# Four groups of layer-two weights kept in DRAM as float32, low parts reordered, and one head's load moved ahead

## The chip, the cores and the metric

The kernel runs on one core of a Trainium2 chip. Its engines have queues of their own, and each works its queue in order: PE (TensorE, matmuls; PEld is its weight loading), DVE (VectorE), ACT (ScalarE), POOL (GpSimd), and SP (SyncE), which issues nearly all DMAs here. The metric is the time of one execution on the device in microseconds (us), the median of several runs.

## The reference

Attention with a decay over 4 batches of 8 heads, 576 positions and 64 values a head, then two feed-forward layers over the 2304 tokens:

```python
scores = scale * q @ k.T + (cum[:, None] - cum[None, :])     # cum: cumulative sum of log(f), causal
x = softmax(scores) @ v                                       # (2304, 512)
h = x @ w_in;   x = (h * clip(h + 3, 0, 6) / 6) @ w_out       # layer one, w_in 512 x 2048
h = x @ w_in2;  y = (max(h, 0) + alpha * min(h, 0)) @ w_out2  # layer two
```

The weights of both layers arrive as float64 bit patterns (two 32-bit words for each number), everything else as float32; the output is float32.

## The kernel before

**Layout.** The hidden width of 2048 is cut into 8 groups of 256; the tokens into three parts of 768 (`p` = 0, 1, 2). A *set* is one layer, one group and one part (`sets`, lines 619 to 625). In each layer the sets with p = 0 and 1 come first, group by group, and then the eight sets with p = 2 in the order 6, 7, 0 to 5. These last eight are the "last third" of a layer.

**A set in steps.** The order inside a set is written out by hand. `SEQ` (line 597) is a string: a digit is one of seven products of a Strassen scheme (`product`, six matmuls each) of this set's tokens with the input weights, a `q` is one `piece` (six matmuls) of the set before with the output weights. A layer-one set has 15 steps, a layer-two set 13. The sums of products and the activation (`activate`: ACT, DVE, ACT and POOL in turn) follow one or two steps later. PSUM holds two tiles for the products of bank A and one each for B and C, so a product waits until ACT (line 687) or DVE (line 690) has read the one before.

**High and low parts.** Matmuls work on a rounded float32 form. Each operand is a pair: the high part is a rounding copy on ACT, the low part is what the copy lost, a subtraction on POOL or DVE. For input weights that is line 176 (`high`) and line 180 (`low`), in four blocks named a, b, c, d (a: columns 0 and 1, used by the products 1 and 7; c: 4 and 5; d: 6; b: 2 and 3), for output weights o0 and o1. For the activations it is line 226 and line 231 (`build_parts`): seven blocks 0 to 6, some of which are sums made on line 223. The products use the blocks in the order 0, 3, 6, 2, 4, 1, 5.

**Conversion of the weights.** A group has four slices (two of input, two of output weights) of 128 x 512 numbers. `fetch` (line 114) brings the raw 512 KB. Then come `m` (magnitude, ACT, line 132), `f`, `s`, `j`, `g` (floor, shift, join, sign; DVE, lines 135 to 148) which make a float32 slice in one of three buffers (`wa`, `wb`, `wc`); `S1` to `S4` (POOL, line 162) make the Strassen sums, and `h..` and `l..` the high and low parts; `wi0` to `wo1` store both to DRAM (line 185), from where the last third loads them (`load_w`, lines 208 and 210). `sign` issues the fetch two slices on.

**Side work by tables.** The strings `CONV_...` and `BUILD` give each of these a step. `side_work` (line 739) is called at the start of a set and queues them with `aside`; in each step the products' own work comes first, then the side work due. The weights of a layer-two group are converted during the two sets of the group before it by `CONV_EVEN`, shifted by 3 steps: 26 steps in all. Those of its first group are converted by `CONV_A` and `CONV_TURN` in the last sets of layer one and the first of layer two.

**The start.** `load_head` brings q and k of one head (608 KB, three buffers) and, for even heads, v. `ak_d` and `aq_d` are copies in DRAM of the rows that carry the decay; from head 2 on `prep_head` reads them back (lines 295 and 296).

Of the kernel before, what the change touches and what calls it, by code (L numbers as in the profile page):

```python
# [21 lines left out]
def decay_attention_ffn2_kernel(ctx, tc, qk, v, f, wi1, wo1, wi2, wo2, alpha, out):  # L22
    nc = tc.nc
# [15 lines left out]
    KT = 5  # L39
    TAIL = S - 512  # L40
# [9 lines left out]
    CONV_EVEN = "m0 0 f0 1 s0 2.5 j0 4 g0 5.5 m1 5 f1 7 s1 8.5 j1 10 g1 11.5 S1 12 S2 13 hc 14 S3 14 hb 15 lc 15 lb 16 ha 16 S4 17 m2 18 hd 18 f2 19 ld 19 s2 20 la 20 j2 21 m3 21 g2 22.5 f3 23 ho0 23 lo0 24 s3 24.5 j3 26 g3 27 ho1 28 lo1 29 wi0 40 wi1 43 wo0 46 wo1 48"  # L50
    CONV_TURN = "S1 11 S3 12 S2 13 hb 30 ha 30 hc 31 lb 32 la 33 S4 34 lc 35 m2 38 hd 37 ld 38 f2 41 s2 42 j2 43 g2 44 m3 42 f3 46 s3 47 j3 48 g3 49 ho0 47 lo0 49 ho1 51 lo1 52 wi0 58 wi1 61 wo0 64 wo1 66"
# [27 lines left out]

    aq_d = dram.tile([2, 32, 4, QW], F32, name="aq_d")  # L80
# [35 lines left out]
    def conv_ops(ff, g):  # L116
# [3 lines left out]
        def f32(s):  # L120

            if s not in stage:
                tag = {0: "wa", 1: "wb", 2: "wc", 3: "wb", "S": "wc"}[s]
                stage[s] = wtmp.tile([128, KH, 256], F32, tag=tag, name=tag)
            return stage[s]
# [60 lines left out]

        for s in range(4):
            for name, fn in (("m", magnitude), ("f", floor), ("s", shift), ("j", join), ("g", sign)):
                ops[f"{name}{s}"] = lambda fn=fn, s=s: fn(s)
# [53 lines left out]
    def build_ops(k, p, add, subs):  # L243
        adds, highs, lows = build_parts(k, p, add, subs)
        return [(t, {"h": highs, "l": lows, "a": adds}[name[0]][int(name[1]), c])
# [14 lines left out]
    def attention():  # L260
        with ExitStack() as ax:
# [239 lines left out]
            for a in range(2):  # L501
                nc.sync.dma_start(out=ak_d[a, 0:NP], in_=ak[32 * a:32 * a + NP].bitcast(F32))
            prep_head(1)
# [14 lines left out]
            load_head(3)  # L518
# [220 lines left out]
    def side_work(s):  # L739
# [8 lines left out]
        def build(k, pair, subs, add=nc.vector, even=None):  # L748
            for i, (t, fn) in enumerate(build_ops(k, pair, add, subs)):
                aside(t if even is None else even[0] + i / even[1], fn)  # L750
# [10 lines left out]
        if p == 0 and (1 if ff else 2) <= g + 1 < NG and not (ff == 0 and g < 2):  # L761
            ops, keep = conv_ops(ff, g + 1), g + 1 < NG - 2
            for text in ((CONV_EVEN,) if ff else (CONV_A, CONV_B)):
                conversion(ops, text, keep, 1, 3 if ff else 5)
        if p == NPR - 1:
# [8 lines left out]
            if ff == 0 and j == NG - 3:  # L774
                early["second"] = conv_ops(1, 0)
                conversion(early["second"], CONV_A, True)
# [104 lines left out]
```

## Time and profile before

| | |
|---|---|
| median of 3 runs | 1024.52 us (1023.65 to 1025.59) |
| the profiled execution | 1023.57 us, of which its span is 1021.8 us |
| PE busy | 966.4 us (95%) |
| DVE, ACT, POOL busy | 739.2 (72%), 588.5 (58%), 589.0 (58%) us |
| mean granted clock of PE | 0.992 of full |
| DMA | 139.18 MB, mean 136 GB/s |

Attention takes about the first 240 us, layer one lasts until about 604 us, layer two until the end. Busy time counts an engine's own work only; a wait shows as idle time, put down to the engine that ended it. PEclk is the granted clock: 1.00 is the higher of its two levels (2.4 GHz), 0.50 the lower (1.2 GHz).

### The profile page before, as it was taken

To read this page: it belongs to the slowest core of one execution; us is meant where nothing else is said; L and a number is where in the kernel's file an instruction comes from. 1 tells how busy PE (TensorE), PEld (TensorE's weight loads), DVE (VectorE), ACT (ScalarE), POOL (GpSimd) and SP (SyncE) were. 2 spreads that over 40 slices of the span, in tenths; PEclk is the share of its full clock that TensorE was granted. 3 is DMA by queue.
4 is the path that set the end of the run, shared out by engine and by line. 5 is a ranking of instruction groups with operands and counts; after the bars stand their busy time and mean duration, and the time that the engine had idled before them with its cause. 6 is when DMAs were issued, how large, how long until landed. Compare 5 with 4: busy or idle time off the path is not lost.

```text
span 1021.8 us, 15850 instructions
## 1 busy us (share of the span) xinstructions
PE 966.4 (95%) x5488; PEld 862.7 (84%) x5488; DVE 739.2 (72%) x1284; ACT 588.5 (58%) x1444; POOL 589.0 (58%) x577
## 2 busy tenths in 40 slices
PE   4999999998999999999999997999999999999998
PEld 3666666678899999998999996888888888888987
DVE  6787987857688788878345668677887778735454
ACT  4677787776555555554544354766555556564452
POOL 7467578856655656566555377565556556532221
PEclk9899999999999999999999998999999999999999
DMA  7555576501424444210254513344244420244531
GB/s 206 178 173 153 173 241 212 149 6 42 155 71 169 181 171 181 94 43 1 76 223 179 203 53 104 131 166 175 85 174 163 167 83 0 94 170 160 226 144 73
DMA packets 32260, 139.18 MB, mean 136 GB/s; under 512 B 4156, under 2 KB 4156, under 8 KB 29044
## 3 DMA queue, kind: packets, MB, share of 16 engines
q1 hardware_dynamic: 32176, 138.17, 39.0%
q8 instruction: 43, 0.70, 0.3%
q14 instruction: 37, 0.30, 0.1%
q10 hardware_dynamic: 4, 0.00, 0.0%
HBM read 94.06 MB, written 39.94 MB: 131 GB/s over the span
## 4 chain that ended last, share of the span: by engine, by line
PE 71%; DVE 15%; POOL 5%; ACT 4%; issue 3%; DMA 1%; SPq 1%; ACTq 0%; DVEq 0%; POOLq 0%
PE o L715 17%; PE o L713 16%; PE hA L682 16%; PE hC L682 9%; PE pv L436 4%; PE hB L682 4%; DVE nm L323 3%; PE tp L379 2%; PE sc L346 2%; POOL wi L180 2%; POOL g L665 1%; DVE nm L325 1%; DVE r L223 1%; ACT g L664 1%; PE sc L347 1%
## 5 line engine op out<-in xcount | busy, mean ns | idle before, releaser
L682 PE MATMUL hA<-xh,wi 128*128 128x384 f32 x768 | 227.1, 341 | 22.2 <-POOL wi L180 11.2
L713 PE MATMUL o<-g,wo 128*128 128x384 f32 x1152 | 232.3, 340 | 1.2 <-POOL g L665 1.2
L715 PE MATMUL o<-wo,g 128*128 128x512 f32 x864 | 224.1, 395 | 1.8 <-POOL g L665 1.4
L665 POOL TENSOR_TENSOR g<-t,g 128x384 fp32r<-128x384 f32 x120 | 127.7, 1065 | 162.2 <-ACT g L664 142.5
L713 PEld LDWEIGHTS o<-g,wo 128*128 128x128 f32 x1152 | 205.8, 189 | 2.1 <-POOL g L665 1.8
L715 PEld LDWEIGHTS o<-wo,g 128*128 128x128 f32 x864 | 160.5, 188 | 29.0 <-POOL g L665 2.7
L682 PEld LDWEIGHTS hA<-xh,wi 128*128 128x128 f32 x768 | 142.1, 189 | 29.8 <-POOL wi L180 13.5
L665 POOL TENSOR_TENSOR g<-s,g 128x384 fp32r<-128x384 f32 x72 | 75.8, 1053 | 155.3 <-ACT g L664 144.9
L733 DVE TENSOR_TENSOR r<-o,r 128x512 f32<-128x512 f32 x126 | 86.5, 687 | 64.0 <-PE o L715 62.9
L682 PE MATMUL hA<-xl,wi 128*128 128x384 f32 x384 | 130.4, 340 | 2.1 <-POOL xl L231 2.1
L722 DVE SCALAR_TENSOR_TENSOR r<-o,r 128x384 f32<-128x384 f32 x168 | 91.4, 551 | 50.5 <-PE o L713 50.1
L664 ACT CAST g<-t 128x384 fp32r<-128x384 f32 x120 | 61.7, 514 | 107.4 <-DVE t L656 89.2
L682 PE MATMUL hC<-xh,wi 128*128 128x384 f32 x384 | 114.3, 338 | 1.3 <-ACT s L687 1.3
L331 ACT ACTIVATE p<-sc,nm 128x128 f32<-128x128 f32 (+4 forms) x160 | 84.5, 531 | 21.3 <-DVE nm L325 9.9
L323 DVE TENSOR_REDUCE nm<-sc 128x1 f32<-128x128 f32 (+4 forms) x160 | 71.5, 469 | 10.5 <-PE sc L348 7.8
L231 POOL TENSOR_TENSOR xl<-r,xh 128x384 fp32r<-128x384 f32 x65 | 74.8, 1168 | 5.1 <-ACT xh L226 4.9
L682 PEld LDWEIGHTS hA<-xl,wi 128*128 128x128 f32 x384 | 72.7, 189 | 5.4 <-POOL xl L231 2.3
L664 ACT CAST g<-s 128x384 fp32r<-128x384 f32 x72 | 37.0, 514 | 65.9 <-DVE s L659 65.1
L682 PEld LDWEIGHTS hC<-xh,wi 128*128 128x128 f32 x384 | 71.1, 188 | 3.8 <-ACT s L687 1.6
L687 ACT COPY s<-hA 128x384 f32<-128x384 f32 x96 | 45.9, 478 | 44.3 <-PE hA L682 44.2
L379 PE MATMUL tp<-ident,p 128*128 128x128 f32 x384 | 69.4, 285 | 0.6 <-ACT pt L395 0.6
L346 PE MATMUL sc<-k,q 128*128 128x256 f32 (+2 forms) x128 | 55.9, 437 | 11.6 <-DVE k L314 9.4
(128 smaller groups left out, 1927.2 us busy)
## 6 DMA issues: line engine op xcount, KB each, us to landing
wid<-wi SPq DMA_DIRECT2D x24, 896.0 KB
wi<-wid SPq DMA_DIRECT2D x12, 1792.0 KB
rqk<-in_qk SPq DMA_DIRECT2D x32, 608.0 KB
raw<-in_wi SPq DMA_DIRECT2D x32, 512.0 KB
raw<-in_wo SPq DMA_DIRECT2D x32, 512.0 KB
wod<-wo SPq DMA_DIRECT2D x24, 512.0 KB
wo<-wod SPq DMA_DIRECT2D x12, 1024.0 KB
vt<-in_v SPq DMA_DIRECT2D x16, 320.0 KB
```

Source lines behind the costliest of these rows:

```text
L231: e.tensor_sub(out=XS[k][1][:, b, c], in0=x, in1=XS[k][0][:, b, c].bitcast(F32))
L323: nc.vector.tensor_reduce(out=nm[:, i:i + 1], in_=src, axis=AX.X, op=ALU.max, negate=True)
L331: nc.scalar.activation(out=pt[:, c0:c0 + cw], in_=src, func=AF.Exp, bias=nm[:, 0:1], scale=1.0, accum_out=dsts[i])
L346: nc.tensor.matmul(out=sc[:, 0:n], lhsT=q1[:, qs], rhs=k1[:, 0:n], start=True, stop=False)
L379: nc.tensor.transpose(tp[:, j, :], pt[:, 128 * j:128 * j + 128], ident)
L664: nc.scalar.copy(out=gt[n][i][:, 0], in_=hold["g"])
L665: nc.gpsimd.tensor_sub(out=gt[n][i][:, 1], in0=hold["g"], in1=gt[n][i][:, 0].bitcast(F32))
L682: nc.tensor.matmul(out=h, lhsT=a, rhs=b[:, x, kc], start=new and kc + e == 0, stop=kc == KH - 1 and e == 2, skip_group_check=not new)
L713: nc.tensor.matmul(out=o[:, 0:NB], lhsT=a[:, cs], rhs=b, start=st, stop=sp)
L715: nc.tensor.matmul(out=o, lhsT=b[:, cs], rhs=a, start=st, stop=sp)
L722: later(0, lambda: nc.vector.scalar_tensor_tensor(out=acc, in0=o[:, 0:NB], scalar=1.0 / 6.0, in1=acc, op0=ALU.mult, op1=ALU.add))
L733: nc.vector.tensor_add(out=acc, in0=o, in1=acc)
```

## The change

1. In the last third of layer one, from its first set on, sixteen slices of layer two (groups 0 to 3, `NC` = 4) are converted, a slice in six steps, and stored as float32 in a new DRAM buffer `f_d` (`c0` to `c3`); the three buffers are taken in turn.
2. For these four groups `CONV_TURN` now begins with loads of those slices (`p0` to `p3`) on SP in place of the conversion, and goes on with sums, high and low parts as before. For group 0 it is queued in the last set but one of layer one.
3. `CONV_EVEN` (layer-two groups 4 to 7) runs its first slices up to 1.5 steps closer together, and the high and low part of block a come before b instead of last (`ha` 13 for 16, `la` 15 for 20).
4. Two of the builds of activations take a new order (`BUILD_FIRST`): block 6 directly after its sum, ahead of 4 and 1.
5. The load of head 3 is issued directly after the copies `ak_d`, ahead of the copies `aq_d` and of the preparation of head 1, and no longer after them.

```diff
@@ -37,6 +37,7 @@
     KT = 5
+    NC = 4
     TAIL = S - 512
@@ -47,8 +48,9 @@
     CONV_B = "hb 11 S1 11 S3 12 lb 13 S2 13 S4 14 ha 14 hc 16 la 16 hd 17 lc 18 ld 19 m2 19 f2 20 s2 21 j2 22 g2 23 m3 21 f3 24 s3 25 j3 26 g3 27 ho0 25 lo0 27 ho1 29 lo1 31 wi0 40 wi1 43 wo0 46 wo1 48"
-    CONV_EVEN = "m0 0 f0 1 s0 2.5 j0 4 g0 5.5 m1 5 f1 7 s1 8.5 j1 10 g1 11.5 S1 12 S2 13 hc 14 S3 14 hb 15 lc 15 lb 16 ha 16 S4 17 m2 18 hd 18 f2 19 ld 19 s2 20 la 20 j2 21 m3 21 g2 22.5 f3 23 ho0 23 lo0 24 s3 24.5 j3 26 g3 27 ho1 28 lo1 29 wi0 40 wi1 43 wo0 46 wo1 48"
-    CONV_TURN = "S1 11 S3 12 S2 13 hb 30 ha 30 hc 31 lb 32 la 33 S4 34 lc 35 m2 38 hd 37 ld 38 f2 41 s2 42 j2 43 g2 44 m3 42 f3 46 s3 47 j3 48 g3 49 ho0 47 lo0 49 ho1 51 lo1 52 wi0 58 wi1 61 wo0 64 wo1 66"
+    CONV_EVEN = "m0 0 f0 1 s0 2 j0 3.5 g0 5 m1 4 f1 6.5 s1 8 j1 9 g1 10 S1 11 S2 12 S3 12 hc 13 ha 13 lc 14 hb 14 la 15 lb 16 S4 17 m2 18 hd 18 f2 19 ld 19 s2 20 j2 21 m3 21 g2 22.5 f3 23 ho0 23 lo0 24 s3 24.5 j3 26 g3 27 ho1 28 lo1 29 wi0 40 wi1 43 wo0 46 wo1 48"
+    CONV_TURN = "p0 0 p1 0 S1 6 S2 7 S3 7 hc 8 ha 8 lc 9 hb 9 la 10 lb 11 S4 12 hd 13 ld 14 p2 14 p3 15 ho0 24 lo0 25 ho1 26 lo1 27 wi0 40 wi1 43 wo0 46 wo1 48"
+    BUILD_FIRST = "h0 l0 a3 h3 l3 h2 l2 a4 a6 h6 l6 h4 l4 h1 l1 a5 h5 l5"
     BUILD = "h0 2 l0 4 a3 6 h3 9 l3 11 h2 9 l2 11 a4 13 a6 15 h4 16 l4 18 h1 17 l1 19 h6 19 l6 21 a5 22 h5 26 l5 28"
@@ -77,6 +79,7 @@
+    f_d = [dram.tile([128, 4, KH * 256], F32, name=f"fd{g}") for g in range(NC)]
     aq_d = dram.tile([2, 32, 4, QW], F32, name="aq_d")
@@ -113,7 +116,7 @@
-    def conv_ops(ff, g):
+    def conv_ops(ff, g, cache=False):
@@ -121,6 +124,8 @@
                 tag = {0: "wa", 1: "wb", 2: "wc", 3: "wb", "S": "wc"}[s]
+                if cache:
+                    tag = ("wa", "wb", "wc")[(4 * g + s) % 3]
                 stage[s] = wtmp.tile([128, KH, 256], F32, tag=tag, name=tag)
@@ -184,7 +189,16 @@
+        def saved(s, put):
+            t = f32(s).rearrange("p k n -> p (k n)")
+            if put:
+                nc.sync.dma_start(out=f_d[g][:, s], in_=t)
+            else:
+                nc.sync.dma_start(out=t, in_=f_d[g][:, s])
+
         for s in range(4):
+            ops[f"c{s}"] = lambda s=s: saved(s, True)
+            ops[f"p{s}"] = lambda s=s: saved(s, False)
             for name, fn in (("m", magnitude), ("f", floor), ("s", shift), ("j", join), ("g", sign)):
@@ -240,8 +254,12 @@
-    def build_ops(k, p, add, subs):
+    def build_ops(k, p, add, subs, even=None):
         adds, highs, lows = build_parts(k, p, add, subs)
+        if even is not None:
+            fns = [{"h": highs, "l": lows, "a": adds}[name[0]][int(name[1]), c]
+                   for name in BUILD_FIRST.split() for c in range(KH)]
+            return [(even[0] + i / even[1], fn) for i, fn in enumerate(fns)]
         return [(t, {"h": highs, "l": lows, "a": adds}[name[0]][int(name[1]), c])
@@ -500,6 +518,7 @@
                 nc.sync.dma_start(out=ak_d[a, 0:NP], in_=ak[32 * a:32 * a + NP].bitcast(F32))
+            load_head(3)
             prep_head(1)
@@ -515,7 +534,6 @@
                 nc.sync.dma_start(out=aq_d[a, 0:NP], in_=aq[32 * a:32 * a + NP].bitcast(F32))
-            load_head(3)
             nc.gpsimd.tensor_scalar(out=alpha_sb, in0=alpha_sb, scalar1=-1.0, scalar2=None, op0=ALU.mult)
@@ -746,8 +764,8 @@
         def build(k, pair, subs, add=nc.vector, even=None):
-            for i, (t, fn) in enumerate(build_ops(k, pair, add, subs)):
-                aside(t if even is None else even[0] + i / even[1], fn)
+            for t, fn in build_ops(k, pair, add, subs, even):
+                aside(t, fn)
@@ -760,8 +778,9 @@
             ops, keep = conv_ops(ff, g + 1), g + 1 < NG - 2
-            for text in ((CONV_EVEN,) if ff else (CONV_A, CONV_B)):
-                conversion(ops, text, keep, 1, 3 if ff else 5)
+            cached = ff == 1 and g + 1 < NC
+            for text in ((CONV_TURN if cached else CONV_EVEN,) if ff else (CONV_A, CONV_B)):
+                conversion(ops, text, keep, 1, 3 if ff and not cached else 5)
         if p == NPR - 1:
@@ -771,12 +790,15 @@
                 build(1, 0, (nc.gpsimd,), nc.gpsimd, (0, 0.7))
-            if ff == 0 and j == NG - 3:
-                early["second"] = conv_ops(1, 0)
-                conversion(early["second"], CONV_A, True)
-                conversion(early["second"], CONV_TURN, True, last=15)
+            if ff == 0 and j == 0:
+                for k in range(4 * NC):
+                    if k % 4 == 0:
+                        ops = conv_ops(1, k // 4, True)
+                    for i, name in enumerate("mfsjgc"):
+                        aside(6 * k + (0, 1, 2, 3, 4, 5)[i], ops[f"{name}{k % 4}"])
+            if ff == 0 and j == NG - 2:
+                conversion(conv_ops(1, 0), CONV_TURN, True, 1, 7)
             if ff == 0 and j == NG - 1:
-                conversion(early["second"], CONV_TURN, True, 1, -30, 30)
                 build(0, 1, (nc.gpsimd, nc.vector), nc.gpsimd)
```

## Rows read from the trace of the kernel before

**Rows 1.** The page, its part 1: busy us (share) xinstructions.
```profile
PE 966.4 (95%) x5488; PEld 862.7 (84%) x5488; DVE 739.2 (72%) x1284; ACT 588.5 (58%) x1444; POOL 589.0 (58%) x577
```

**Rows 2.** Waits of PE: waiter and releaser, us in total, times, longest.
```profile
PE hA L682 <- POOL wi L180: 11.2, 7, 1.9
...
PE hA L682 <- DVE s L690: 7.7, 2, 5.7
PE sc L347 <- DMA k<-ak_d: 5.3, 1, 5.3
...
PE hA L682 <- POOL xl L231: 2.1, 1, 2.1
```

**Rows 3.** Windows, most cut at sets; busy (instructions), granted clock, DMA share, GB/s.
```profile
320.00:460.00 140.00, 140.00 (x799) 140.00 (x798) 117.29 (x203) 73.51 (x145) 83.91 (x79) 1.00 0.36 130
380.00:400.00 20.00, 20.00 (x115) 20.00 (x115) 18.84 (x34) 10.31 (x21) 9.34 (x9) 1.00 0.23 79
477.70:493.50 15.80, 15.80 (x92) 15.80 (x91) 8.49 (x17) 7.37 (x15) 6.89 (x8) 1.00 0.04 8
525.10:540.90 15.80, 15.80 (x92) 15.80 (x91) 8.15 (x15) 7.37 (x16) 10.20 (x11) 1.00 0.44 183
556.70:572.50 15.80, 15.80 (x92) 15.80 (x91) 12.28 (x23) 6.02 (x12) 4.49 (x5) 1.00 0.66 250
588.30:603.90 15.60, 15.60 (x91) 15.60 (x90) 9.06 (x16) 9.56 (x21) 11.49 (x12) 1.00 0.20 67
603.90:630.60 26.70, 18.60 (x92) 17.31 (x92) 25.44 (x34) 12.56 (x27) 21.78 (x18) 0.87 0.26 83
646.30:680.00 33.70, 31.90 (x156) 27.79 (x155) 25.26 (x37) 23.52 (x50) 20.10 (x18) 1.00 0.38 136
680.00:713.45 33.45, 31.54 (x157) 28.11 (x156) 26.83 (x43) 19.67 (x42) 19.25 (x18) 1.00 0.41 151
848.00:864.00 16.00, 14.35 (x71) 12.56 (x70) 14.35 (x19) 8.24 (x18) 9.89 (x9) 1.00 0.00 0
```

**Rows 4.** The chain that ended last: two sets of layer two's end; start, us.
```profile
898.19 2.12 PE hA L682 x12
...
913.97 2.10 PE hA L682 x12
```

**Rows 5.** Windows around the waits at the start and at 258 us.
```profile
16.00:19.50 3.50, 3.50 (x18) 2.64 (x18) 2.16 (x5) 1.75 (x9) 3.42 (x4) 1.00 0.88 111
19.50:25.00 5.50, 1.81 (x15) 1.33 (x14) 2.73 (x4) 3.13 (x13) 2.00 (x4) 1.00 0.94 327
20.90:26.60 5.70, 0.41 (x4) 0.21 (x3) 1.88 (x3) 1.73 (x8) 3.26 (x4) 0.97 0.96 282
26.60:33.20 6.60, 6.57 (x28) 5.58 (x29) 3.64 (x10) 3.37 (x11) 4.16 (x5) 0.50 0.58 197
258.30:262.90 4.60, 4.58 (x17) 4.58 (x18) 3.74 (x8) 1.31 (x3) 1.62 (x2) 0.63 0.11 35
```

**Rows 6.** SP's queue in order of time, start of the kernel: start, us, DMA.
```profile
12.23 0.84 SPq L502 DMA_DIRECT2D ak_d<-ak  x2
...
16.01 1.46 SPq L277 DMA_DIRECT2D rqk<-in_qk  x1
...
20.08 0.36 SPq L296 DMA_DIRECT2D k<-ak_d  x1
```

**Rows 7.** POOL in order of time, around 254 us and at a group's end.
```profile
254.51 3.76 POOL L231 TENSOR_TENSOR xl<-r,xh 128x384 fp32r<-128x384 f32 x3
...
681.11 1.71 POOL L180 TENSOR_TENSOR wi<-wa,wi 128x512 fp32r<-128x512 f32 x1
```

**Rows 8.** Groups by shape, 320 to 460 us: count, busy us, mean ns, idle before.
```profile
L143 DVE SCALAR_TENSOR_TENSOR wb<-raw,wb 128x512 uint32<-128x512 uint32 x9 | 9.3, 1030 | 0.0
...
L143 DVE SCALAR_TENSOR_TENSOR wa<-raw,wa 128x512 uint32<-128x512 uint32 x4 | 2.7, 675 | 0.0
```

**Rows 9.** DVE in order of time, before the second set of layer one.
```profile
240.29 1.55 DVE L148 SCALAR_TENSOR_TENSOR wb<-raw,wb 128x512 uint32<-128x512 uint32 x1
```

## The prediction, made before the changed kernel was run

> **What bounds the kernel now.** First the page: TensorE (PE) is busy 966.4 of the 1021.8 us span [rows 1], the others 58 to 72%. So time can come only from TensorE's 55.4 us of idleness and from stretches at the low clock, and the question is where they lie. The waits of PE by what ended them give the places [rows 2]: 11.2 us in seven waits for a low part of an input weight (POOL, line 180), 5.7 us in one wait for a DVE addition, 5.3 us in one for a small DMA at the start, 2.1 us for a low part of an activation.
>
> Then windows cut at the sets of the schedule [rows 3]. In an undisturbed layer-one set PE is busy 15.80 of 15.8 us. The first set of layer two takes 26.7 us, with DVE busy 25.44 of them. A pair of layer-two sets takes 33.45 us while weights are converted, where the chain of waits shows 913.97 - 898.19 = 15.78 us for a set without conversion [rows 4], so 31.56 for a pair. The clock is read in short windows [rows 5]: it is granted at half for 6.6 us after the wait at the start, and at 0.63 on average for 4.6 us after the wait at 258 us. Between 380 and 400 us DVE is busy 18.84 of 20, 94%, and PE still waits for nothing; in the sets from 477.7 to 588 PE doesn't wait either, and DVE is little over half busy [rows 3]: that is the room into which work is moved.
>
> **The change, part by part.**
>
> *Head 3 asked for sooner.* Its load is issued at 16.01, after the copies of aq, and two fetches of raw weights follow; the 9 KB that PE waits for (k from ak_d) are issued at 20.08 [rows 6]. PE stands from 20.9 to 26.6 [rows 5], 5.3 us of it for that transfer [rows 2]. Between 16 and 19.5 the DMA engines move 111 GB/s [rows 5]. The load can be issued at 12.23 + 0.84 = 13.07, 2.9 us sooner, and fill that stretch. But the copies of aq now queue behind its 608 KB, and the small loads of head 2 wait for those copies as before. Bounds: nothing, if the small load still lands last behind the same bytes; or the whole 5.3 plus the half of 6.6 us that the low clock costs, 8.6. I take 2.6 of the wait (most of the 2.9) and 0.9 of the clock, because PE will still wait some us there: 3.5 gained. A loss is excluded: ACT's first copy of transposed scores (line 390) waits until aq has landed, and that comes up to 608 KB later, 1.9 us at the 327 GB/s that the DMA moves from 19.5 to 25 [rows 5]; it lies inside the wait that is there now. POOL's preparation of head 3 is already done before PE needs it and only gets earlier.
> By the Trainium skill, DMA: Bandwidth & Descriptors, section "Queues, rings and completion order", descriptors are taken in the order of their ring on each DMA engine; by that rule the small load stays behind the raw weights whatever is reordered ahead of it, and this term would be 0. The trace agrees so far, as 9 KB issued at 20.08 end a wait at 26.6.
>
> *Low parts of the built activations in order of use.* PE waits 2.1 us [rows 2] for xl; POOL does three of them in a row from 254.51 to 258.27 [rows 7]. The seventh block is the third that the products use; its low part moves ahead of four other names of the list, that is 4 x 2 / 1.5 = 5.3 steps of 1.05 us. Bounds: the wait alone, 2.1, or with the clock after it, 0.37 x 4.6 = 1.7, together 3.8. I take 3.5, since 5.3 steps are more than the wait. What becomes late next are the blocks now behind it, used four and more steps later.
>
> *Conversion out of the turn between the layers.* The first set of layer two takes 26.7 instead of 15.8 us: 10.9 lost. In it DVE is full [rows 3], with the conversion of about three slices, half of the low parts of the next activations and its own work; PE's wait of 5.7 us is for DVE [rows 2]. After the change no slice is converted there: the four slices of a group come back as float32 from DRAM, four DMAs of 256 KB on SP, and DVE loses some 12 of its 25 us (three slices of four instructions, about 1 us each [rows 8]). What is late next is POOL: it is busy 11.49 + 21.78 = 33.3 us in these two sets [rows 3], and keeps nearly all of it, in 31.6 us if PE loses nothing; three sums of 0.7 us and the next group's begin are added, less what POOL loses now beside DVE. So some 2 to 3 us of overflow. I leave 2.9 and gain 8; bounds 3 (POOL and late loads take most of it) and 10.9.
>
> *Order of the low parts in layer two.* The seven waits are each for the low part of blocks 0 and 1 ("la"), which the first product of a group needs and which POOL does last, for 1.71 us from 681.11 [rows 7]; the longest of the waits is 1.9 us [rows 2]. In groups 4 to 7 la goes from step 23 to 18 of 26, five steps or 6 us sooner against a wait of 1.9; in groups 1 to 3, which come from DRAM, to step 15. The part of block 6 gets up to 1.7 us later, but is first needed by the fourth product. Lost now: 33.7 - 31.6 = 2.1 once, 33.45 - 31.56 = 1.9 five times, 1.65 in the last [rows 3], 13.2 in all. I leave 0.2 a group for other small waits and gain 12; bounds 8 (another part late by half) and 13.2. The squeezed conversion of groups 4 to 7 has DVE busy as now (26.83 of 33.45, then of 31.6, 85%).
>
> *What is added to the last third of layer one.* Sixteen slices, one in six steps, so 2.5 in a set: for each one ACT instruction (ACT is busy 6 to 7.4 us of a set here [rows 3]), four of DVE, a store of 256 KB, and the 512 KB fetch that comes sooner. DVE's price for a slice from two places [rows 3]: the set from 556.7 converts two, (12.28 - 8.15) / 2 = 2.1; from 320 to 460 there are 117.29 us in 8.86 sets, 13.24 a set, with 17 slices (one kind of step stands in [rows 8], nine and four times, and four times more on a third tile), 1.92 a set, so (13.24 - 8.15) / 1.92 = 2.65. With 2.5 slices that is 5.3 to 6.6 us on a base of 8.15 to 8.49: at most 15.1 of 15.8. The cover is thin, 96% where 94% is shown without a wait. If it is gone, PE waits as at the turn. Bounds 0 and 4 (some 0.7 us a set); I take 1. DMA: a set's weights, 2.75 MB, take 0.44 of 15.8 us = 7.0 us [rows 3]; 1.9 MB more make that 11.8. Two of the fetches come right behind such a load and may be 1 us late for their ACT instruction; the queue behind it on ACT is half empty, so nothing. SP has only these transfers to issue. The stores' buffer comes round after three slices, 18 steps.
> The Trainium skill, SBUF — State Buffer, section "Who interferes with whom", says that a DVE instruction with two SBUF inputs, or in a two-port mode, and a GpSimd instruction shut each other out for the whole of the other's length. The rows agree: the same conversion step took 675 ns with one tile and 1030 with another [rows 8]. By the rule a slice could wait for four POOL instructions, and the term would go to the bound of the rival below.
>
> **Sum.** 3.5 + 3.5 + 8 + 12 - 1 = 26 us. The profiled execution: 1021.8 - 26 = 995.8 span, and with the 1.8 us around it (its time is 1023.57) 997.6. The median of the runs, 1024.52, is 0.95 above that execution: 998.5.
>
> **Rivals.**
> (a) POOL takes DVE's place at the turn and the last third pays for thin cover: 3 instead of 8, -4 instead of -1: 18 gained, 1006.5. For it: 33.3 us of POOL work in 31.6. Against: that count holds POOL's time lost beside DVE. 17 in 100.
> (b) In layer two another part is late in la's place, so half of 12 comes: 1004.5. For it: POOL works the parts one after another. Against: 6 us of shift against 1.9. 10 in 100.
> (c) The start gives nothing, being bound by bytes: 1002. 10 in 100.
> (d) Slower: DVE fills in the last third. The longest such instruction that I found took 1.55 us [rows 9]; four of that length make 6.2 a slice, 99 for sixteen, on a base of 6 x 8.15 = 49 in the first six sets, against 95 available: 53 over, less 27 gained elsewhere, 1050.5. It decides from (95 + 27 - 49) / 16 = 4.6 us a slice. Against: 2.1 to 2.65 measured beside the same neighbours. 5 in 100.
> (e) The order in the text doesn't reach the engines, since they wait for something else than their place: the waits stay and the conversion moved was hidden anyway: within 0.2% of 1024.5. Against: the turn's DVE is on the chain. 3 in 100.
>
> **Numbers.** The forecast has 55 in 100, alone 992 to 1004. All gains at their upper bounds and no cost: 8.6 + 3.8 + 10.9 + 13.2 = 36.5, 988; (a) and (b) together 1012.5. With (d) and (e) left out the range 989 to 1010 leaves about 2 in 10. A measurement of this kernel can tell some 0.2% from no change, 2 us. Faster is the forecast with (a), (b), (c): 92; within 3; slower 5.
>
> **What would show it.** Right: no PE wait for POOL line 180 in layer two and pairs of 31.6 to 32; the first set of layer two at 16 to 19 us; PE 15.8 of 15.8 in the last third with DVE at 13 to 15; the wait at 258 us gone; PE going on at about 24 instead of 26.6 at the start. Wrong: PE waits for DVE additions from 480 to 590 us, or a new wait for S1 to S4 behind the loads before 590, or POOL g ending PE's waits at the turn.

## The result, and the profile after

Sets are named (layer, group, part), counted from 0 as in the code: (1, 0, 0) is the first set of layer two. Line numbers of the changed kernel are 5 to 18 above those of before: products at 700 (before: 682), pieces at 731 and 733, ScalarE's copy of a product at 705 (687), VectorE's addition at 708 (690), low parts at 185 (180) and 245 (231).

The changed kernel takes 1015.27 us (median of 4, 1012.13 to 1015.96), before 1024.52; ratio 0.9903, interval 0.9881 to 0.9926. The gain is 9.25 us where 26 were forecast, and the time lies above the range. The profiled execution is the shortest of the four, 1012.13 with a span of 1010.3, 11.5 under the span of before.

The page's part 1 shows the same work: PE is as busy as in [rows 1], in a shorter span.

```profile
PE 965.5 (96%) x5488; PEld 859.7 (85%) x5488; DVE 735.9 (73%) x1284; ACT 589.1 (58%) x1444; POOL 590.0 (58%) x577
```

The waits of PE, to be read beside [rows 2] (waiter and releaser, us in total, times, longest). First two of before that [rows 2] leaves out:

```profile
PE hA L682 <- ACT s L687: 3.1, 3, 1.6
...
PE hC L682 <- ACT s L687: 1.3, 1, 1.3
```

and those of the changed kernel:

```profile
PE hA L700 <- ACT s L705: 5.4, 6, 1.6
PE sc L365 <- DMA k<-ak_d: 3.9, 1, 3.9
PE hC L700 <- ACT s L705: 3.6, 3, 2.6
PE o L733 <- POOL g L683: 3.0, 5, 1.2
...
PE hA L700 <- DVE s L708: 2.1, 1, 2.1
PE o L731 <- POOL g L683: 2.0, 4, 0.6
...
PE hA L700 <- ACT g L682: 1.4, 1, 1.4
```

The three kinds that the change aimed at have gone: the 11.2 us for a weight's low part, the 5.7 for a DVE addition, the 2.1 for xl. What has grown are the waits for ScalarE's copy s of a product, from 4.4 us in four to 9.0 in nine, and those for a result g on GpSimd, from 2.6 us in five to 5.0 in nine.

Windows cut at the sets, beside [rows 3]: two sets of the last third, (0, 5, 2), (1, 0, 0), (1, 0, 1) and two pairs of layer two.

```profile
521.40:538.30 16.90, 16.43 (x91) 15.73 (x91) 15.04 (x25) 9.24 (x19) 10.18 (x10) 1.00 0.85 310
538.30:556.60 18.30, 16.82 (x92) 15.56 (x91) 17.61 (x29) 8.22 (x17) 11.48 (x11) 1.00 0.64 246
588.30:608.60 20.30, 17.65 (x92) 17.33 (x91) 8.94 (x16) 9.13 (x20) 14.09 (x15) 0.92 0.36 116
608.60:625.70 17.10, 16.25 (x91) 15.61 (x90) 12.30 (x20) 9.54 (x21) 17.10 (x16) 1.00 0.14 51
625.70:646.00 20.30, 16.56 (x80) 13.95 (x80) 5.69 (x10) 13.38 (x28) 15.79 (x16) 1.00 0.32 123
646.00:677.50 31.50, 31.50 (x157) 28.27 (x156) 12.73 (x21) 21.02 (x44) 18.53 (x19) 1.00 0.32 118
677.50:709.00 31.50, 31.50 (x158) 28.39 (x157) 16.17 (x26) 17.22 (x36) 18.16 (x18) 1.00 0.31 115
```

Layer two's first pairs stand at the floor of 31.5 us. The first set of layer two has fallen from 26.7 to 17.1, but the sets on either side of it have grown from 15.8 to 20.3 each. Taken from the first matmul of each set to that of the next, the profiled executions of the two kernels differ so:

| stretch | before, us | after, us | gained | forecast |
|---|---|---|---|---|
| first matmul and first set, with attention | 230.04 | 227.18 | 2.9 | 3.5 |
| (0, 1, 0) to (0, 1, 1): build order | 55.03 | 54.08 | 0.95 | 3.5 |
| (0, 7, 1) and (0, 0, 2) to (0, 2, 2): conversion added | 65.93 | 69.93 | -4.0 | -1 |
| turn: (0, 5, 2), (1, 0, 0), (1, 0, 1) | 58.28 | 57.69 | 0.6 | 8 |
| (1, 1, 0) to the end | 371.68 | 360.56 | 11.1 | 12 |

The sets not named differ by 0.05 in all; the sum is 11.5. The terms of the start and of layer two's order came about as forecast. The turn gave almost nothing, and two smaller terms were mis-sized by 2.5 and 3. Each of these stretches is taken from one execution of each kernel.

What happens at the turn begins on SP, in order of time:

```profile
575.28 0.50 SPq L222 DMA_DIRECT2D wi<-wid  x1
579.57 0.33 SPq L117 DMA_DIRECT2D raw<-in_wi  x1
579.95 0.49 SPq L195 DMA_DIRECT2D fd<-wa  x1
588.12 0.32 SPq L197 DMA_DIRECT2D wa<-fd  x1
588.48 0.43 SPq L197 DMA_DIRECT2D wb<-fd  x1
```

and goes on in the chain that ended last (start, us, what):

```profile
579.95 8.15 DMA fd<-wa
...
588.12 3.05 DMA wa<-fd
591.17 1.79 issue
592.96 0.74 POOL wc L167
```

The sixteenth slice is stored from the buffer `wa`, which the first slice of group 0 needs next. That store of 256 KB is issued behind 2.75 MB of weight loads (574.86 and 575.28) and 512 KB of raw weights (579.57), and takes 8.15 us from its issue to its landing; only then can SP ask for the slices. The Trainium skill, DMA: Bandwidth & Descriptors, section "Queues, rings and completion order", says that each DMA engine takes descriptors in the order of their ring; the 8.15 us agree with it. The chain names no cause for the 1.79 us after the first slice; the sum also reads the second one, `wb`, asked for at 588.48. GpSimd's first sum starts at 592.96, and ScalarE, in order of time, stands before the cast of its result with a copy that PE needs behind it:

```profile
595.41 0.62 ACT L181 CAST wi<-wc 128x512 fp32r<-128x512 f32 x1 [5.37 <-POOL wc L167]
...
597.97 0.47 ACT L705 COPY s<-hC 128x384 f32<-128x384 f32 x1
```

PE in order of time, at the turn; the brackets are its waits:

```profile
598.49 0.46 PE L700 MATMUL hC<-xh,wi 128*128 128x384 f32 x1 [2.65 <-ACT s L705]
...
628.62 1.20 PE L733 MATMUL o<-wo,g 128*128 128x512 f32 x4 [1.25 <-POOL g L683]
...
633.62 0.44 PE L700 MATMUL hA<-xh,wi 128*128 128x384 f32 x1 [1.34 <-ACT s L705]
...
639.92 0.44 PE L700 MATMUL hA<-xh,wi 128*128 128x384 f32 x1 [1.15 <-ACT s L705]
```

The first is the only wait of PE in (0, 5, 2) from 586 to 606 us. After it the granted clock is 0.54 on average from 598.5 to 602 us, near the lower of its levels, which by estimate costs some 0.46 x 3.5 = 1.6 us; with the 2.65 us of the wait that is nearly all of the 4.4 us that the set lost. The last three lie in (1, 0, 1): GpSimd is busy all 17.10 us of the set before and 15.79 in this one (windows above), and ScalarE stands once more, 4.16 us before the cast `hd` of a sum that GpSimd does last:

```profile
639.08 0.40 ACT L181 CAST wi<-wb 128x256 fp32r<-128x256 f32 x1 [4.16 <-POOL wb L167]
639.39 0.47 ACT L705 COPY s<-hA 128x384 f32<-128x384 f32 x1
```

### The profile page after: what moved, and what is told of

Read it like the earlier page. It is cut to its first block, busy times and chain, and to the rows that moved or that the text cites. A ratio compares the mean times of both kernels' runs of the same rounds, so it can differ in the third digit from the quotient of the medians.

```text
span 1010.3 us, 15919 instructions
## 1 busy us (share of the span) xinstructions
PE 965.5 (96%) x5488; PEld 859.7 (85%) x5488; DVE 735.9 (73%) x1284; ACT 589.1 (58%) x1444; POOL 590.0 (58%) x577
## 4 chain that ended last, share of the span: by engine, by line
PE 57%; DVE 23%; POOL 7%; ACT 6%; issue 4%; DMA 2%; SPq 0%; POOLq 0%; ACTq 0%; DVEq 0%
PE o L733 13%; PE hA L700 12%; PE o L731 12%; PE hC L700 7%; PE pv L454 4%; PE hB L700 3%; DVE nm L341 3%; PE tp L397 2%; DVE t L674 2%; PE sc L364 2%; POOL wi L185 2%; POOL g L683 1%; DVE r L751 1%; DVE s L708 1%; ACT g L682 1%
## 5 line engine op out<-in xcount | busy, mean ns | idle before, releaser
L700 PEld LDWEIGHTS hA<-xh,wi 128*128 128x128 f32 x768 | 142.0, 188 | 15.1 <-ACT s L705 7.6
L245 POOL TENSOR_TENSOR xl<-r,xh 128x384 fp32r<-128x384 f32 x65 | 78.5, 1225 | 4.1 <-ACT xh L240 3.7
L700 PE MATMUL hC<-xl,wi 128*128 128x384 f32 x192 | 65.1, 339 | 0.0
## 6 DMA issues: line engine op xcount, KB each, us to landing
wo<-wod SPq DMA_DIRECT2D x12, 1024.0 KB
```

What stands on the lines that cost most here:

```text
L245: e.tensor_sub(out=XS[k][1][:, b, c], in0=x, in1=XS[k][0][:, b, c].bitcast(F32))
L700: nc.tensor.matmul(out=h, lhsT=a, rhs=b[:, x, kc], start=new and kc + e == 0, stop=kc == KH - 1 and e == 2, skip_group_check=not new)
```

## The experiments

Times are medians; "before" ran on the same chip at 1023.3 to 1024.0. The second set begins 227.0 to 229.4 us into the span with the same work ahead of it, so kernels whose times differ by less than some 1.5 us are told apart by their sets, not by the whole.

**again.** The changed kernel once more.

> The changed kernel once more, to have it beside the others on one chip, and a second trace of it. Its profiled execution took 1012.1 us where the three others took 1015.1 to 1016.0. If the 3 us between them come from how late the small load of head 2 lands or how often the clock falls, the set from 588 us (the last of layer one) keeps its 20.3 us and the two sets after it 37.4 together; if they come from the crowded turn itself, those three sets (57.7 us in the first trace) take up to 3 us longer.

1013.07 us, ratio 0.9894 (0.9881 to 0.9908). The turn's three sets take 22.24, 16.30 and 20.25 us, 58.8 in all, 1.1 more than in the first trace: the loss there repeats, (0, 5, 2) being 2.0 us longer and (1, 0, 0) 0.9 shorter. No execution was as slow as the 1015 to 1016 us of three of the first four, so where those 3 us lay stays open.

**turn_buffers.** The slices use the buffers in another rotation, so that the last store doesn't hold `wa`.

```diff
-                    tag = ("wa", "wb", "wc")[(4 * g + s) % 3]
+                    tag = ("wa", "wb", "wc")[(4 * g + s + 2) % 3]
```

> One thing altered in the changed kernel: the three buffers are taken in another order, so that the sixteenth slice lies in the buffer that the turn needs last, and the first two loads of the turn don't wait for its store. Theory 'store': in the trace the load of slice 0 stood from 580 until 588.1 us, when that store (issued at 580, behind 2.75 MB of weights) had landed; ACT then stood 5.4 us in front of a high part, and PE 2.65 us and 3.4 us at the low clock. Then the last set of layer one falls from 20.3 us to 16 to 17.5, and the time by 2 to 4 us. Rival 'bytes': the two loads still run behind the same 2.75 MB and land 1 us sooner at most; the set stays within 0.7 us of 20.3. Rival 'POOL': the set gets shorter, but the two sets after it give it back, since POOL has the same work in less time; the three together stay at 57 to 58.

1010.33 us, ratio 0.9863 (0.9848 to 0.9878). SP in order of time: the loads follow the last store at once, and are issued 6.2 us sooner than in the changed kernel.

```profile
581.45 0.43 SPq L195 DMA_DIRECT2D fd<-wc  x1
581.92 0.43 SPq L197 DMA_DIRECT2D wa<-fd  x1
```

(0, 5, 2) takes 16.37 us in place of 20.28 and 22.24; (1, 0, 0) gives 1.6 to 2.4 back and (1, 0, 1) keeps its 20.25. The late store is shown to be the cause of the first loss, and of 2.3 to 3.4 us net of the turn. Only part of the 6.2 us arrives, though: GpSimd's first sum starts 1.7 us sooner, since the load of the second slice, itself behind the weights, lands 8.9 us after its issue at 582.39. The rival "bytes" was right in this, and wrong that it would leave the set as it was.

```profile
591.26 0.75 POOL L167 TENSOR_TENSOR wc<-wa,wb 128x256 f32<-128x256 f32 x1 [1.50 <-DMA wb<-fd]
```

**turn_adds_dve.** The additions of the second pair's build go from GpSimd to VectorE.

```diff
-                build(0, 1, (nc.gpsimd, nc.vector), nc.gpsimd)
+                build(0, 1, (nc.gpsimd, nc.vector), nc.vector)
```

> One thing altered in the changed kernel: the eight additions of the build at the turn (line 237) go from POOL to DVE. Theory 'POOL': POOL is busy 17.7 and 19.3 of 20 us from 600 to 640, and PE's waits there (1.25 and 1.34 and 1.15 and four small ones) end on POOL or on ACT standing behind it; without 8 to 9 us of additions the sets from 608.6 and 625.7 take 32 to 34 us together and not 37.4, and the time falls by 3 to 5 us. Rival 'DVE': DVE, with 8 more instructions, is what is late again, and the two sets stay above 36. The set from 588 keeps its 20 us in both.

1015.77 us, ratio 0.9920 (0.9908 to 0.9932). (1, 0, 0) and (1, 0, 1) take 39.3 us in place of 37.4. The window of (1, 0, 0), and PE in order of time:

```profile
608.60:628.40 19.80, 16.91 (x92) 15.61 (x91) 18.62 (x28) 9.87 (x21) 13.90 (x11) 1.00 0.16 61
```

```profile
616.75 0.44 PE L700 MATMUL hA<-xh,wi 128*128 128x384 f32 x1 [1.61 <-ACT s L705]
...
635.89 0.45 PE L700 MATMUL hA<-xh,wi 128*128 128x384 f32 x1 [2.00 <-ACT s L705]
```

GpSimd has 13.90 of 19.8 us now and VectorE 18.62: the filling moves from one engine to the other, as the rival "DVE" said. So it isn't enough to relieve GpSimd; the work of the build has to find room on both.

**order_only.** The kernel before with the new `CONV_EVEN` alone, in groups 1 to 7.

```diff
-    CONV_EVEN = "... hc 14 S3 14 hb 15 lc 15 lb 16 ha 16 S4 17 ... ld 19 s2 20 la 20 j2 21 ..."
+    CONV_EVEN = "... S3 12 hc 13 ha 13 lc 14 hb 14 la 15 lb 16 S4 17 ... ld 19 s2 20 j2 21 ..."
```

> One part of the change alone on the kernel before: the new order in CONV_EVEN, which here serves groups 1 to 7; no slice is kept in DRAM, the turn, the start and the builds are as before. Theory: the seven waits for the low part of block a were worth 13 us and nothing of that hangs on the slices in DRAM: 1024.5 - 11 to 13 = 1011.5 to 1013.5, so by itself faster than or equal to the whole change, and the pairs of layer-two sets take 31.6 to 32.5 us. Rival: in the first three groups it is the conversion taken away that frees PE; with the order alone groups 1 to 3 keep half or more of their waits, and the time is 1016 to 1019.

1016.45 us, ratio 0.9929 (0.9917 to 0.9942): 7.6 us from the reordered table alone. The waits of PE from 660 to 880 us hold none for a low part of a weight any more; what is left:

```profile
PE o L715 <- POOL g L665: 2.5, 6, 0.7
PE o L715 <- ACT g L664: 0.8, 2, 0.4
```

So the rival's reason is not there, although the time lies in its range and the theory's 1011.5 to 1013.5 is missed. The first sets of groups lose their 1.6 to 2.2 us of waiting. The second sets take some 0.7 us more from the third group converted in a row on (0.35 in (1, 2, 1), 0.95 in (1, 7, 1)), with these waits for g, and (1, 0, 1) takes 1.05 more. That is a part of rival (b), some 40% of a group's gain in the later groups.

**start_only.** The kernel before with the load of head 3 moved, alone.

```diff
                 nc.sync.dma_start(out=ak_d[a, 0:NP], in_=ak[32 * a:32 * a + NP].bitcast(F32))
+            load_head(3)
...
-            load_head(3)
```

> The kernel before with one edit alone: load_head(3) moved ahead, as in the changed kernel. Theory 'start': the first set, with the attention, takes 217 to 219 us instead of 220.64, the rest of the sets keep their durations, and the time is 1021 to 1023 us (before: 1024.5). Rival 'no start': the gain at the start was chance, 1024 to 1025.5 us.

1021.77 us (12 executions), ratio 0.9977 (0.9967 to 0.9988): 2.1 us. In the fifteen profiled executions with the moved load the second set begins at 228.4 us on average (227.0 to 229.4), in the two with the old place at 230.04 and 231.12: 2.2 us. The window from 16 to 19.5 us now moves 329 GB/s where [rows 5] has 111:

```profile
16.00:19.50 3.50, 3.50 (x19) 3.16 (x18) 2.36 (x7) 1.54 (x6) 3.13 (x4) 1.00 1.08 329
```

One thing in this trace wasn't expected: the three sets (0, 1, 0) to (0, 1, 1), whose build has the old order here, take 54.14 us together, 0.9 less than the 55.03 of the kernel before. So the 2.1 us need not all lie at the start.

**two_groups** and **one_group.** turn_buffers with two groups and one group kept in DRAM.

```diff
-    NC = 4
+    NC = 2          # one_group: 1
```

> turn_buffers with two groups kept in DRAM instead of four, groups 2 and 3 converted in layer two by the order of the even groups. Theory 'overlap': the loss of 3.7 us in the last third comes from the slices that are converted beside POOL's build of layer two's first pair (they run on to 580 us with four groups, to about 527 with two): the sets at 521 and 538 us fall from 16.9 and 18.2 to about 16 each, and groups 2 and 3 lose at most 1 us together against turn_buffers, so the whole is 1.5 to 3 us faster than turn_buffers (1007.5 to 1009). Rival 'groups': groups 2 and 3 need their stored weights; their sets take 1.7 to 2 us more each and eat the gain: 1010 to 1012.

> turn_buffers with one group alone kept in DRAM. Theory 'overlap': the last third takes what it took in the kernel before (15.8 us a set), and the second set of layer two, which in order_only lost only 1.05 us with group 1 converted beside it, takes 17 instead of 20.25 us, because POOL and ACT are no longer asked for group 1's sums within 10 us; group 1's own set loses 1 us: 1004 to 1007. Rival 'groups': with the DVE again converting group 1 in the first set of layer two, next to the build of the second pair, that set takes 20 us or more instead of 18.7, and the whole is 1008 to 1011.

two_groups: 1007.73 us, ratio 0.9846 (0.9829 to 0.9862), within what theory "overlap" gave for the time; of its two sets (0, 2, 2) falls as it said and (0, 1, 2) doesn't. Windows of (0, 1, 2) and (0, 2, 2):

```profile
521.80:538.70 16.90, 16.42 (x92) 15.84 (x92) 13.23 (x23) 10.02 (x21) 12.63 (x12) 1.00 0.72 268
538.70:554.40 15.70, 15.70 (x91) 15.70 (x91) 8.00 (x15) 6.63 (x14) 8.21 (x10) 1.00 0.47 185
```

Without slices to convert, (0, 2, 2) stands at 15.76 us; the 2.4 us were their price. (0, 1, 2) still has a slice and still loses 1.0. Groups 2 and 3 are converted without a loss, in the sets (1, 1, 0) to (1, 2, 1), which stay at 15.8; but the 0.7 us that second sets lose from the third group converted in a row on begin two groups sooner, and that gives 1.5 us back.

one_group: 1010.48 us, ratio 0.9868 (0.9850 to 0.9885). Both theories hold in their own place: the last third has no loss and (1, 0, 1) takes 17.64, but (1, 0, 0), with VectorE converting group 1 beside the build, takes 22.54 with a wait of 3.40 us for a DVE addition. Two groups are the better number.

**group1_later**, **two_late_hd**, **two_later.** Three ways to take group 1's work out of GpSimd's full stretch; a place is one step of the tables, about 1.2 us in layer two (13 steps in 15.78 us). group1_later is turn_buffers, the others two_groups, with

```diff
# group1_later (shift 9); two_later (shift 8)
-                conversion(ops, text, keep, 1, 3 if ff and not cached else 5)
+                conversion(ops, text, keep, 1, 9 if ff and g == 0 else 3 if ff and not cached else 5)
# two_late_hd
-    CONV_TURN = "... S4 12 hd 13 ld 14 p2 14 p3 15 ..."
+    CONV_TURN = "... S4 12 p2 14 p3 15 hd 18 ld 19 ..."
```

> turn_buffers with group 1's table of work begun 4 places later, nothing else. Theory 'POOL full': the second set of layer two (20.25 us) waits because group 1's sums and low parts come on POOL while it is still building the second pair; later, they fall behind that build: the set takes 16 to 18 us, and less than 1 us comes back in the next set: 1007 to 1009. Rival 'total': POOL has the same work in the same three sets and the loss only moves into group 1's set: 1010 to 1011.

> two_groups with one cast on ScalarE and the low part behind it (hd and ld) moved five places later in the table of the groups kept in DRAM, nothing else. Theory 'head of line': the second set of layer two (20.28 us) loses its last wait because ScalarE stands 4.2 us before hd, with PE's copies of hA and hC queued behind it, while GpSimd does three low parts before S4; the wait of 1.14 us at 633.87 and the copies' delay go, the set takes 18.0 to 19.3 us, the time is 1006 to 1007. Rival 'POOL full': GpSimd is full there and the wait goes to its own sums (POOL g): the set stays above 19.8 us and the time at 1007.5 to 1008.

> two_groups with group 1's table begun 3 places later in the set (not 4, since its last store must come ahead of group 2's first step). If the two gains add, as they should when they lie in different sets: last third as in two_groups, second set of layer two 17.5 to 18 us as in group1_later, 1004.5 to 1006. Rival: the group 2 conversion by the order of the even groups collides with the late low parts of group 1 and the sets of groups 1 and 2 give 1 us or more back: 1006 to 1008.

| kernel | us | ratio | (1, 0, 0) | (1, 0, 1) | (1, 1, 0) |
|---|---|---|---|---|---|
| turn_buffers | 1010.33 | 0.9863 | 18.73 | 20.25 | 15.77 |
| group1_later | 1009.27 | 0.9864 (0.9846 to 0.9882) | 18.69 | 17.53 | 16.01 |
| two_groups | 1007.73 | 0.9846 | 17.72 | 20.28 | 15.77 |
| two_late_hd | 1007.43 | 0.9846 (0.9831 to 0.9861) | 17.84 | 18.89 | 15.77 |
| two_later | 1006.96 | 0.9842 (0.9827 to 0.9857) | 17.71 | 19.07 | 15.77 |

In group1_later, PE in order of time has one wait left in (1, 0, 1):

```profile
628.11 1.21 PE L733 MATMUL o<-wo,g 128*128 128x512 f32 x4 [1.25 <-POOL g L683]
```

Four places later take 2.7 us from the set and give 0.2 back in the next: the work collided, it wasn't too much in all. This is read from the sets; the whole times don't show it (ratio 0.9864 beside 0.9863). Moving `hd` and `ld` alone takes 1.4: the last of the three waits was ScalarE standing before `hd`, as theory "head of line" has it. Three places later take 1.2, not the 2.3 to 2.8 that I expected, and the times of the last three kernels differ by less than their spread.

**old_order**, **conv_later**, **first_adds_pool.** two_later with, in the second and third set of layer one and the one after, (1) block 6 behind blocks 4 and 1 again, (2) group 2's conversion three places later, (3) the build's additions on GpSimd.

```diff
# old_order
-    BUILD_FIRST = "... a4 a6 h6 l6 h4 l4 h1 l1 a5 h5 l5"
+    BUILD_FIRST = "... a4 a6 h4 l4 h1 l1 h6 l6 a5 h5 l5"
# conv_later
-            conversion(ops, CONV_A, True, 1, 1)
+            conversion(ops, CONV_A, True, 1, 4)
# first_adds_pool
-            build(1, 1, both, even=(1, 1.5))
+            build(1, 1, both, nc.gpsimd, (1, 1.5))
```

> two_later with the old order of the build (h6 and l6 behind l1 again), nothing else. Theory 'order': the three sets from 228 to 282 us, 54.05 us in two_later, take again what they take in the kernel before, 55.0 us: the order alone is worth 1 us, and the time is 1007.5 to 1008.5. Rival 'cover': the old order's wait for xl was in the shadow of VectorE's backlog, which is the same in both; the three sets stay within 0.4 us of 54.05.

> two_later with the first half of group 2's conversion begun 3 places later in the set at 247 us, nothing else. Theory 'backlog': VectorE stands late there because the conversion comes on top of the last additions of the build (it runs back to back from 251 to 266 us and PE then waits 1.95 us at 264.5 for ACT g behind it); 3 places later the additions are done first, the wait at 264.5 shrinks by more than half, and the three sets together take 52.3 to 53.3 us in place of 54.05: 1005.3 to 1006.5. Rival 'build alone': the wait comes from the build's own work on VectorE and GpSimd, and the sets stay within 0.4 us, or the conversion collides with its second half (54.5 or more).

> two_later with the additions of build(1,1), which run on VectorE at 222 to 278 us, given to GpSimd (the build order and its pace stay). Theory 'backlog': the waits that the new order left there (2.1 us for DVE s near 243, 1.4 us for ACT g near 263) come from VectorE, which has the additions on top of the conversion: the three sets from 228 to 282 us, 54.0 us in two_groups and 53.8 to 54.1 in the others, take 51 to 52.5 us, and the time is 1.5 to 2.5 us under two_later. Rival 'GpSimd': its two thirds of the low parts and the 16 additions fill it, and the wait for xl comes back: 54 us or more, no gain.

The three sets (0, 1, 0), (0, 0, 1) and (0, 1, 1) take 54.05 us in two_later, 55.06 in old_order (1006.69 us, 0.9842, 0.9819 to 0.9865), 52.56 in conv_later (1004.50 us, 0.9822, 0.9809 to 0.9836) and 57.19 in first_adds_pool (1010.23 us, 0.9868, 0.9852 to 0.9885). PE in order of time, in two_later:

```profile
244.46 0.44 PE L700 MATMUL hA<-xh,wi 128*128 128x384 f32 x1 [2.10 <-DVE s L708]
...
264.48 0.41 PE L700 MATMUL hA<-xh,wi 128*128 128x384 f32 x1 [1.95 <-ACT g L682]
```

in old_order, where the wait for xl is back and the one at 264 is not there:

```profile
256.95 0.45 PE L700 MATMUL hA<-xl,wi 128*128 128x384 f32 x1 [2.09 <-POOL xl L245]
```

and in first_adds_pool, where the wait for a sum g on GpSimd has grown:

```profile
251.39 2.02 PE L731 MATMUL o<-g,wo 128*128 128x384 f32 x10 [1.87 <-POOL g L683]
```

The window of (0, 0, 1) in two_later, then in conv_later:

```profile
246.70:265.60 18.90, 16.32 (x92) 15.57 (x90) 16.53 (x28) 10.77 (x23) 11.69 (x10) 1.00 0.08 28
```

```profile
247.10:264.20 17.10, 16.36 (x91) 15.61 (x91) 14.24 (x25) 10.87 (x23) 10.95 (x10) 1.00 0.07 22
```

So the order takes 1.0 us from these sets, although it trades the wait of 2.09 us for xl for one of 1.95 us behind VectorE; the whole times of two_later and old_order don't show it. Nor is it safe as a price of the order: with the old order the sets take 55.03, 55.06 and 55.06 us in three traces, but 54.14 in start_only, where the wait for xl is 1.8 us. With the new order and no other edit to these sets they take 54.02 to 54.08 in ten traces and 54.62 in even_earlier. The wait at 264 comes from the conversion on top of the build: with three places between them it is gone, and of the 1.5 us that the sets gain the next one, (0, 2, 0), gives 0.6 back. Additions on GpSimd make it worse, as the rival "GpSimd" said, though the wait for xl that it named comes back with 0.2 us only.

**even_later** and **even_earlier.** two_later with the table of the even groups one place later and sooner (shift 4 and 2 in place of 3).

> two_later with the table of the even groups begun one place later (shift 4 in place of 3). In groups 2 to 7 the second set takes 16.45 us in place of 15.77 since PE waits 0.35 us twice for a sum g on GpSimd, whose low-part work starts just then. Theory 'phase': the wait depends on where S1 to S3 fall against the four g of a product; one place later it goes, or shrinks by half: 2 to 4 us in all, 1002 to 1003.5. Rival 'load': it is the amount of work; the same 0.7 us a group, in another place: no more than 0.5 us difference from two_later.

> two_later with the table of the even groups begun one place sooner (shift 2 in place of 3). One place later cost 0.45 us in each second set of groups 2 to 7 (16.47 to 16.92). Theory 'phase': one place sooner the two waits of 0.35 us for g on GpSimd fall by half or go, each second set takes 15.8 to 16.2 us, and the time is 1003.5 to 1006. Rival 'either side': the low parts then meet the next product's g instead, as many us or more: 1006.5 to 1009.

1011.04 us (0.9879, 0.9862 to 0.9897) and 1018.98 us (0.9961, 0.9948 to 0.9973). Both miss what theory "phase" gave (1002 to 1003.5 and 1003.5 to 1006). One place later costs 0.4 us in most second sets, one place sooner that and 1.4 to 1.9 us a first set. Waits of PE from 690 to 890 us in even_earlier (two_later: 2.5 us in 6, and 0.8 in 2):

```profile
PE o L733 <- POOL g L683: 5.8, 12, 0.7
PE o L733 <- ACT g L682: 2.4, 6, 0.4
```

The place of this table is the best of the three tried: a step of about 1.2 us costs 4 us one way and 12 the other. Theory "phase" was right that the place decides, but on neither side is there a gain; the rival "either side" was right for one place sooner, with too small a price.

## Why the prediction was wrong, point by point

**The turn is the step that failed** (8 forecast, 0.6 came). The prediction took VectorE's work out of (1, 0, 0) and left 2.9 us for GpSimd's overflow. VectorE's 25.44 us did fall to 12.30 and that set became 9.5 us shorter, within the 16 to 19 us that the prediction gave it as a sign; the sets on either side grew by 4.4 and 4.5. Two things stood in the way. First, "the stores' buffer comes round after three slices, 18 steps" was counted between slices, and not from the last store to the first load; and the store was counted by its bytes alone, though it queues behind 2.75 MB of weights and 512 KB of raw ones. The chain shows 8.15 us, turn_buffers that waiting for this store costs 2.3 to 3.4. The prediction named this sign ("a new wait for S1 to S4 behind the loads before 590") and gave it no price. Second, the overflow is not what a sum of busy time says. GpSimd has 14.09, 17.10 and 15.79 us in the three sets, 47 of 57.7, so it isn't full over the turn; but in the 17.1 us of (1, 0, 0) it has no gap, and the g that PE needs queues in between. ScalarE, with room to spare, passes the delay on, since casts that wait for GpSimd stand ahead of its copies of products. group1_later and two_late_hd show both: the same work some places later gives 2.7 and 1.4 us. That PE's waits for g would end on GpSimd was the other sign that the prediction named.

**The last third** was mis-sized: -4.0 against -1, the bound given. The term that failed is the price of a slice on VectorE, taken as 2.1 to 2.65 us. In (0, 1, 2) and (0, 2, 2) the timeline of VectorE has nine and eleven instructions of the conversion that add up to 7.5 and 9.1 us, 3.3 for the four of a slice, which take 2.2 where GpSimd is idle (0.42, 0.41, 0.68, 0.68); so VectorE is busy 15.04 and then 17.61 us where 15.1 was the most forecast. After 556 us, where GpSimd has no build left, a set with slices to convert holds 15.8, and at more GB/s than in the two sets that lose, so the transfers aren't the cause:

```profile
556.60:572.50 15.90, 15.90 (x92) 15.90 (x91) 13.82 (x27) 7.88 (x15) 4.96 (x5) 1.00 0.89 332
```

The loss lies where slices meet that build, though not in every such set: (0, 0, 2) before them has both (VectorE busy 13.95 and GpSimd 13.15 of 15.9 us from 505.5) and loses 0.1. The same VectorE step beside GpSimd and, at 552.28, with GpSimd idle, in the timeline of the changed kernel:

```profile
541.04 1.37 DVE L674 SCALAR_TENSOR_TENSOR t<-t,s 128x384 f32<-128x384 f32 x1
541.95 1.33 POOL L237 TENSOR_TENSOR r<-r 128x384 f32<-128x384 f32 x1
542.33 1.50 DVE L153 SCALAR_TENSOR_TENSOR wa<-raw,wa 128x512 uint32<-128x512 uint32 x1
...
552.28 0.55 DVE L674 SCALAR_TENSOR_TENSOR t<-t,s 128x384 f32<-128x384 f32 x1
```

1.37 us beside GpSimd, 0.55 alone. The form of this step that takes its second input from PSUM (t<-t,hA) stays at 0.54 to 0.56 in all seven cases from 480 to 590 us, the one at 543.75 beside GpSimd's work among them. The Trainium skill, SBUF — State Buffer, section "Who interferes with whom", which the prediction cited as the rule that speaks against the change, is borne out, and its price should have carried more weight than the mean of other sets. The second half of rival (a), -4, was right here; its own time, 1006.5, was still too low, because the turn gave 0.6 and not 3 and the build's order 0.95 and not 3.5. That the slices cause the loss is shown (two_groups, one_group); that the mutual blocking and not the mere count of instructions does it is read from the timeline and not tested, and (0, 1, 2) in two_groups, which loses 1.0 us with VectorE at only 13.23 of 16.9, speaks for it.

**The build's order** was mis-sized: 0.95 against 3.5, below the bound of 2.1. The wait for xl went; that the next wait would come behind VectorE, 7 us later, wasn't priced. In the old order the wait for xl covers it (old_order). As start_only shows 0.9 us in these sets without the new order, even the 0.95 isn't shown to be the order's.

**The order in layer two** was right: 11.1 against 12. The 0.2 us a group left for other waits were 0.7 to 0.95 in the second sets of groups 5 to 7, and nothing in the groups from DRAM. order_only shows that 7.6 of the whole gain come from the table alone; in this stretch it takes 363.50 us, so 8.2 of the 11.1 are the table's and 2.9 come with the groups from DRAM.

**The start** was right in mechanism and in sign: 2.1 to 2.9 against 3.5, with the reserve said at start_only. PE goes on at 25.06 where 24 was forecast. The gain goes with the 3.5 us in which the DMA engines, busy 0.88 of the time, had moved 111 GB/s [rows 5]; they move 329 in start_only. The rule of the Trainium skill by which the prediction put this term at 0 (DMA: Bandwidth & Descriptors, "Queues, rings and completion order") speaks of order alone; the small load stayed behind the raw weights, and what lay ahead of it got done sooner.

Put together, the table's order (7.6), the start (2.1) and the build's order (1.0, if it is the order's) make 10.7 us, and the whole change 9.25 to 11: the four groups kept in DRAM gave nothing net as they were made. The sets say the same beside order_only: 4.1 lost in the last third, 1.9 gained at the turn and 2.9 in layer two, 0.7 in all. With two groups, the other rotation and a later table for group 1 the kernel takes 1006.96 us, some 6 more; conv_later, at 1004.50 us the fastest here, adds the three places for group 2's conversion, worth 0.9 by its sets. The turn still has 5.3 us above three undisturbed sets (52.6 in two_later against 47.4); what would remove them wasn't tried.

## What to carry to other kernels

Work that is moved off the engine that is full leaves the others' queues as they are: look at the engine that does the next step in order, not at its share of busy time, and ask what stands behind a waiting instruction there. A buffer that is stored and loaded again is free only when its store has landed, and here it landed behind the loads issued ahead of it; count from the last use to the first, at the seam too. And when a change has five parts, run each alone: here one line of a table gave most of the gain, and the largest part of the diff gave none until its seams were mended.

## What the runs showed that I had not expected

A store of 256 KB took 8.15 us behind 2.75 MB of weight loads and 512 KB of raw ones. After a set in which GpSimd was busy for all 17.1 us, the next one lost 4.5 us, with GpSimd busy 78%. One place in a table, about 1.2 us, cost 4 or 12 us over six groups, by its sign. The end of the first set varies by 2.4 us between the traces of kernels with the same start; how much of the spread of the times that is, isn't shown, as one execution of each kernel was traced.
